# Unit zero of a gating stage: bf16 pieces turned by DMA in place of fp32 transposes and products on TensorE

## Chip, cores and metric

The kernel runs on one core of one Trainium2 chip. The metric is the device time of one execution in microseconds, the median of several runs; a profiled execution gives the trace that is read below.

## What is computed

Three stages follow each other: attention with a band and a few global keys, a dense feed-forward layer with SiLU, and a layer of eight experts of which each token uses one.

```python
x = attention(q, k, v, n_global, n_local)          # 2 x 768 tokens, 8 heads of 64 -> 1536 x 512
h = x @ w_in                                       # 512 -> 2048
x = (h * (1.0 / (1.0 + np.exp(-h)))) @ w_out       # 2048 -> 512
logits = x @ w_gate                                # 512 -> 8
e_idx = np.argmax(logits, axis=1)
probs = softmax(logits)
eom = 1.0 / (1.0 + np.exp(-(x @ w_output_gate)))
for e in range(8):
    mask = e_idx == e
    ye = np.maximum(x[mask] @ w1[e], 0.0) @ w2[e]
    out[mask] = probs[mask, e, None] * eom[mask, e, None] * ye
```

The change touches the step in the middle, the gate: the products of x with `w_gate` and `w_output_gate` (16 columns together). They decide by argmax which expert a token goes to, so they are needed with fp32's precision.

## The kernel before

The 1536 tokens are 12 tiles of 128. Two tiles make a unit, `u` = 0 to 5, and the units form five chunks, `CH=[[0,1],[2],[3],[4],[5]]`. The feed-forward layer runs over chunks, and in a chunk over `FB` = 16 slices `f` of the hidden width. The loop at L1091 has one step `g` for each (chunk, slice), 80 in all; a step issues the first product of its slice (`s1_mm`, L353), the activation (tanh on ScalarE at L357, VectorE at L358, a rounded copy on ScalarE at L361, the rest on VectorE at L362), and `LAG` = 2 steps later the second product (`s2_mm`, L373 to L375, the last with the low part of the weights, which for chunks after the first is loaded from DRAM by `load_wol`, L342).

Between these products a step carries pieces of other work, and all engines work through their instructions in the order in which the program wrote them (a schedule by hand):

- attention of later tiles, in slots of one head pair (`slot`): scores (L171), bias and maximum on VectorE (L182), exponentials on ScalarE (L192), a split into two halves (L196, L199), a DMA transpose of the probabilities (L202), and two or three slots later the product with the values, `emit_pv` (L252), into the single bank `pv`. After the last head pair of a tile VectorE copies the global rows of the values (`glob_v`, L163), scales the bank into SBUF (`emit_fin`, L262), and only then may the next tile write the bank. The values are split by ScalarE and GpSimd (L148 to L153);
- the gate of the units of the chunk that has ended, a list `gq` of small functions of which one is run in each step from step 18 on (L1114).

For a unit outside the set `PU` (L418) the list holds `gate1` for each of the two tiles (four fp32 transposes on TensorE, L415, and a copy by ScalarE, L417), `gate2` (fp32 logits on TensorE, L448; argmax on VectorE), `gate3` (rank of a token within its expert, two exponentials L486 and L487, the token's factor) and `gate4` (with `gate3` it scatters the two tiles' rows to DRAM from GpSimd's queue, L498). For a unit in `PU` the activations are split into three bf16 parts: `piece1` casts on ScalarE (L428), `piece2` subtracts on VectorE (L430), `piece3` casts (L432), `piece4` subtracts (L434), `turn` transposes a tile's parts with two DMA transposes on SyncE's queue (L437, L438), two empty entries follow, and `gate2` has 24 bf16 matmuls of 48 columns (L446) and one more reduction (L456). Units zero and one both end with chunk zero, so they stand in the list one after the other; after a unit in `PU` the next unit starts four entries before its end, and entries that meet are run in one step, the older first (L1128 to L1131). Unit one's turns are four entries of one DMA transpose each (L1125).

The parts' buffers are shared: the bf16 pairs are two buffers of tag `wt`, and units zero and one (two and three) share one tile `gx` (L422).

Of the kernel before, what the change touches and what calls it, by code (L numbers as in the profile page):

```python
# [23 lines left out]
def kernel(ctx, tc, qk, v, n_global, n_local, w_in, w_out, wg, w1, w2, out):  # L24
# [107 lines left out]
    def abank(shape,name):  # L132
        tg=atags[0][acnt[0]%len(atags[0])]; acnt[0]+=1
        return ps.tile(shape,F32,tag=tg,name=name,bufs=1)
# [277 lines left out]
    def gate1(n):  # L412
# [2 lines left out]
        for k in range(KC): T.transpose(m[:,k,:],xr[:,k*P:(k+1)*P],ident)  # L415
        x=mp.tile([P,KC,P],F32,tag="wt",name="xtf",bufs=2); xts[n]=x
        A.activation(out=x,in_=m,func=AF.Copy)  # L417
    PU=(1,2,3)  # L418
    gbuf={}; xps={}
    def piece1(u):  # L420

# [13 lines left out]
    def turn(n,part=(0,1)):  # L435
        a,b,r,x=xps[n]
        if 0 in part: S.dma_start_transpose(out=x[:,0:2].rearrange("p a k t -> p (a k) t"),in_=a.rearrange("p a d -> p (a d)"))  # L437
        if 1 in part: S.dma_start_transpose(out=x[:,2],in_=b); xts[n]=x; del xps[n]  # L438
    gsm={}
    glp={}  # L440
    def logits(n):
        if n%2==0: glp[n//2]=abank([P,2,48 if n//2 in PU else 16],"gl")
        x=xts.pop(n)
        if n//2 in PU:
            for i in range(3):
                for k in range(KC): T.matmul(glp[n//2][:,n%2],x[:,i,k,:],wgb[:,k].rearrange("p j e -> p (j e)"),start=(i==0 and k==0),stop=(i==2 and k==KC-1))  # L446
            return
        for k in range(KC): T.matmul(glp[n//2][:,n%2],x[:,k,:],wgs[:,k,:],start=(k==0),stop=(k==KC-1))  # L448
    def gate2(u):
# [4 lines left out]
        s=mp.tile([P,2,48],F32,tag="gsm",name="gsm",bufs=2)  # L454
        if u in PU:
            V.tensor_reduce(out=s[:,:,32:48],in_=g.rearrange("p t (j e) -> p t e j",j=3),axis=AX.X,op=ALU.add)  # L456
# [39 lines left out]
    def gate4(u,t):  # L496
        di,xr=gdi[u]
        G.indirect_dma_start(out=XE[:,:],out_offset=bass.IndirectOffsetOnAxis(ap=di[:,t:t+1],axis=0),in_=xr[:,t,:],in_offset=None,bounds_check=NE*CAP-1,oob_is_err=False)  # L498
# [562 lines left out]
    with tc.manual_schedule():  # L1061
# [27 lines left out]
        def run_gates(k):  # L1089
            for _ in range(min(k,len(gq))): gq.pop(0)()  # L1090
        for g in range(len(steps)+LAG):  # L1091
# [23 lines left out]
            if g>=LAG:  # L1115
                c2,f2=steps[g-LAG]
                s2_mm(c2,f2)
                if f2==FB-1:
# [4 lines left out]
                    for u in CH[c2]:  # L1123
                        seq=[lambda n=n,fn=turn if u in PU else gate1: fn(n) for n in (2*u,2*u+1)]
                        if u==1: seq=[lambda n=n,h=h: turn(n,(h,)) for n in (2,3) for h in (0,1)]  # L1125
                        if u in PU: seq=[lambda u=u,fn=fn: fn(u) for fn in (piece1,piece2,piece3,piece4)]+seq+[lambda: None]*2
                        seq+=[lambda u=u,fn=fn: fn(u) for fn in (gate2,gate3,lambda u: gate4(u,1))]
                        for i,fn in enumerate(seq):  # L1128
                            if at+i<len(gq): gq[at+i]=lambda fs=(gq[at+i],fn): [f() for f in fs]
                            else: gq.append(fn)  # L1130
                        at=len(gq)-(4 if u in PU else 0)  # L1131
                    run_gates(3 if c2==0 else 1)
# [75 lines left out]
```

## Time and profile before

| what | us |
|---|---|
| median of 3 runs | 571.04 (570.72 to 571.72) |
| the profiled execution, whole | 572.04 |
| its span, first to last instruction | 570.3 |

| engine | busy, us | share of the span |
|---|---|---|
| TensorE, matmuls | 555.1 | 97% |
| VectorE | 388.2 | 68% |
| ScalarE | 302.7 | 53% |
| GpSimd | 142.8 | 25% |

Times inside the execution are counted from the first instruction. Chunk zero ends near 144 us; the gate of units zero and one lies between 144 and 220. An instruction's row shows its start, its duration (or that of a merged run of equal ones), engine, line, operation and tiles, and in brackets how long the engine sat idle before it and what ended the idle time. Matmuls are pipelined, so the start of the next group tells better than the duration how long a group held TensorE.

### The profile page before, as it was taken

What the parts mean: (1) busy time and instruction counts of PE and PEld (TensorE: products, weight loads), DVE (VectorE), ACT (ScalarE), POOL (GpSimd) and SP (SyncE); (2) the same over time, 40 slices, a digit from 0 to 9 for tenths busy, and PEclk for the clock granted to TensorE, in tenths of its full rate; (3) what the DMA queues carried; (4) which work ended last, traced back from release to release, by engine and by line L of the source; (5) the groups of instructions that cost most, each with busy time, mean ns of one, the idle gap of its engine ahead of it and who ended that gap; (6) DMA issues with size and microseconds to landing.
All of it is one profiled execution on the core that took longest, in us unless ns stands there. A gap on an engine that the chain in (4) does not pass through costs nothing.

```text
span 570.3 us, 12006 instructions
## 1 busy us (share of the span) xinstructions
PE 555.1 (97%) x4027; PEld 469.6 (82%) x4027; DVE 388.2 (68%) x1143; ACT 302.7 (53%) x819; POOL 142.8 (25%) x193
## 2 busy tenths in 40 slices
PE   9999999999999999999999999999999999999993
PEld 4668998888888788888899998788888888888882
DVE  6996899996467657574735346656774967967950
ACT  7993434443545454434532425736655766877740
POOL 2686444343233323123201010220010110110011
PEclk9999999999999999999999999999999999999998
DMA  6876467796657985765493349309764868768500
GB/s 221 273 245 193 173 210 235 241 306 204 185 155 170 185 205 153 167 153 142 111 185 115 91 127 327 141 21 328 267 206 149 248 200 269 239 213 291 157 20 22
DMA packets 90731, 107.53 MB, mean 189 GB/s; under 512 B 39181, under 2 KB 53517, under 8 KB 90661
## 3 DMA queue, kind: packets, MB, share of 16 engines
q1 hardware_dynamic: 87892, 99.77, 58.8%
q0 software_dynamic: 2192, 6.39, 3.0%
q8 instruction: 33, 0.54, 0.4%
q10 hardware_dynamic: 576, 0.52, 0.3%
q14 instruction: 38, 0.30, 0.2%
HBM read 87.14 MB, written 17.66 MB: 184 GB/s over the span
## 4 chain that ended last, share of the span: by engine, by line
PE 87%; ACT 3%; DMA 3%; DVE 2%; issue 2%; POOL 1%; SPq 1%; POOLq 0%; ACTq 0%; DVEq 0%
PE s L353 21%; PE s L373 8%; PE s L374 7%; PE s L375 7%; PE h L696 7%; PE y L729 4%; PE h L697 4%; PE y L731 4%; PE y L730 4%; PE qkp L171 2%; PE pv L252 2%; PE h L702 2%; PE xy L171 2%; PE y L725 2%; PE px L228 1%
## 5 line engine op out<-in xcount | busy, mean ns | idle before, releaser
L353 PEld LDWEIGHTS s<-xT,wi 128*128 128x128 f32 x1152 | 147.6, 190 | 9.6 <-DVE g L362 3.8
L353 PE MATMUL s<-xT,wi 128*128 128x256 f32 x1152 | 151.6, 283 | 0.5 <-DVE g L362 0.5
L357 ACT ACTIVATE u<-s 128x256 f32<-128x256 f32 x96 | 35.4, 381 | 102.2 <-PE s L353 101.4
L358 DVE SCALAR_TENSOR_TENSOR s<-u,s 128x256 f32<-128x256 f32 x96 | 39.7, 426 | 67.3 <-ACT u L357 67.1
L373 PE MATMUL s<-woh,g 128*128 128x512 f32 x192 | 79.4, 414 | 0.4 <-ACT g L361 0.4
L567 DVE TENSOR_TENSOR uq<-qr,uq 128x512 fp32r<-128x512 f32 x112 | 74.4, 689 | 5.2 <-ACT uq L566 3.2
L374 PE MATMUL s<-woh,g 128*128 128x512 f32 x192 | 75.8, 395 | 0.0
L566 ACT ACTIVATE uq<-qr 128x512 fp32r<-128x512 f32 x112 | 66.6, 625 | 3.1 <-DMA qr<-in_w_dram 3.1
L362 DVE TENSOR_TENSOR g<-s,g 128x256 fp32r<-128x256 f32 x96 | 39.3, 422 | 31.1 <-ACT g L361 28.2
L653 POOL DMA_INDIRECT out_dram<-y,ixt x17 | 19.4, 1143 | 154.7 <-ACT y L742 116.4
L361 ACT ACTIVATE g<-s 128x256 fp32r<-128x256 f32 x96 | 35.6, 381 | 29.8 <-DVE s L358 29.8
L192 ACT ACTIVATE t<-t,mx 128x256 f32<-128x256 f32 (+1 forms) x96 | 46.1, 486 | 0.1
L373 PEld LDWEIGHTS s<-woh,g 128*128 128x128 f32 x192 | 36.3, 189 | 8.5 <-ACT u L357 2.7
L374 PEld LDWEIGHTS s<-woh,g 128*128 128x128 f32 x192 | 36.3, 189 | 5.5 <-DVE g L362 0.5
L375 PE MATMUL s<-wolr,g 128*128 128x512 f32 x128 | 39.8, 392 | 0.8 <-DMA wolr<-wlo_d 0.8
L709 DVE TENSOR_TENSOR h<-h,hs 128x192 f32<-128x192 f32 (+5 forms) x56 | 20.8, 372 | 25.3 <-ACT hs L708 25.2
L729 PE MATMUL y<-uq,hh 128*128 128x512 f32 (+1 forms) x88 | 36.7, 417 | 0.0
L730 PE MATMUL y<-uq,hh 128*128 128x512 f32 (+1 forms) x88 | 34.6, 393 | 0.0
L731 PE MATMUL y<-uq,hh 128*128 128x512 f32 (+1 forms) x88 | 34.6, 393 | 0.0
L711 ACT ACTIVATE hh<-h 128x192 fp32r<-128x192 f32 (+5 forms) x56 | 19.8, 353 | 26.3 <-DVE h L709 15.8
L199 POOL TENSOR_TENSOR hl<-t,hl 128x512 f16<-128x512 f32 (+1 forms) x18 | 19.9, 1105 | 50.4 <-ACT xT L276 16.4
L696 PE MATMUL h<-xwT,uq 128*128 128x448 f32 (+5 forms) x144 | 32.4, 347 | 0.0
(273 smaller groups left out, 1043.4 us busy)
## 6 DMA issues: line engine op xcount, KB each, us to landing
qr<-in_w_dram SPq DMA_DIRECT2D x128, 256.0 KB, 4.3
wolr<-wlo_d SPq DMA_DIRECT2D x64, 256.0 KB, 3.4
wiraw<-in_w_in_dram SPq DMA_DIRECT2D x16, 512.0 KB, 5.2
wraw<-in_w_out_dram SPq DMA_DIRECT2D x13, 512.0 KB, 4.2
ring<-in_qk_dram SPq DMA_DIRECT2D x22, 256.0 KB, 4.2
xe<-xe SPq DMA_DIRECT2D x7, 792.0 KB, 6.7
wlo_d<-wol SPq DMA_DIRECT2D x16, 256.0 KB, 3.0
xw<-xe SPq DMA_DIRECT2D x15, 264.0 KB, 4.7
```

Of the source, the lines that this page charges most:

```text
L192: A.activation(out=t[:,j,:ce],in_=t[:,j,:ce],func=AF.Exp,scale=-1.0 if 4*n<SB else 0.125,bias=mx[n][:,h:h+1],accum_out=ss[n][:,h,0:1])
L353: T.matmul(t,w[:,ww,kc,:],x[:,xx,kc,:],start=(k==0),stop=(k==11)); k+=1
L358: V.scalar_tensor_tensor(out=t,in0=u,scalar=1.0,in1=t,op0=ALU.add,op1=ALU.mult)
L373: T.matmul(o,g[u][:,0,sl],wh,start=(f==0),stop=False)
L374: T.matmul(o,g[u][:,1,sl],wh,start=False,stop=False)
L375: else: T.matmul(o,g[u][:,0,sl],wl,start=False,stop=(f==FB-1))
L566: A.activation(out=t[:,0],in_=r,func=AF.Copy)
L567: (G if (i%2 if pool is None else pool) else V).tensor_tensor(out=t[:,1],in0=r,in1=t[:,0],op=ALU.subtract)
L696: for kc in range(KC): T.matmul(t[:,:2*W],uq[4*p+2*(f//4),kc][:,0,s],xwT[p,kc][:,:,:W],start=(kc==0),stop=False)
L729: T.matmul(o,hi,w[:,0],start=(f==0),stop=False)
L730: T.matmul(o,g[:,z:z+n],w[:,0],start=False,stop=False)
L731: T.matmul(o,hi,w[:,1],start=False,stop=(f==7))
```

## The change

Unit zero joins the set `PU`. `turn` takes the place of `gate1` for its two tiles, its logits are the 24 bf16 matmuls, and the list of entries is built by the same lines as for the other units of the set. Units four and five keep the fp32 form.

```diff
-    PU=(1,2,3)
+    PU=(0,1,2,3)
```

The lines that read the set, unchanged:

```python
if u in PU: seq=[lambda u=u,fn=fn: fn(u) for fn in (piece1,piece2,piece3,piece4)]+seq+[lambda: None]*2
...
at=len(gq)-(4 if u in PU else 0)
```

## Rows read from the trace of the kernel before

**Rows 1.** Page, part 1: busy time, share of the span, instructions.

```profile
PE 555.1 (97%) x4027; PEld 469.6 (82%) x4027; DVE 388.2 (68%) x1143; ACT 302.7 (53%) x819; POOL 142.8 (25%) x193
```

**Rows 2.** Timeline of PE, unit zero's transposes and logits: start, us, engine, line.

```profile
145.61 0.66 PE L415 MATMUL gt<-ident,xr 128*128 128x128 f32 x4
146.03 0.48 PE L373 MATMUL s<-woh,g 128*128 128x512 f32 x1
...
153.28 1.96 PE L448 MATMUL gl<-wgs,xtf 128*128 128x16 f32 x16
155.09 0.48 PE L373 MATMUL s<-woh,g 128*128 128x512 f32 x1
```

**Rows 3.** Timeline of PE, unit one's bf16 logits.

```profile
207.62 0.76 PE L446 MATMUL gl<-wgb,gx 128*128 128x48 bf16 x24
208.23 0.48 PE L373 MATMUL s<-woh,g 128*128 128x512 f32 x1
```

**Rows 4.** Timeline of DVE: unit one's piece2, first and next after gate2, gate3.

```profile
171.62 1.28 DVE L430 TENSOR_TENSOR gx<-xr,xpa 128x512 f32<-128x512 f32 x2
...
210.06 0.25 DVE L456 TENSOR_REDUCE gsm<-gl 128x32 f32<-128x96 f32 x1
...
211.80 0.43 DVE L358 SCALAR_TENSOR_TENSOR s<-u,s 128x256 f32<-128x256 f32 x1
...
213.91 0.17 DVE L479 TENSOR_TENSOR gsm<-gr,geb 128x16 f32<-128x16 f32 x1
...
215.59 0.43 DVE L358 SCALAR_TENSOR_TENSOR s<-u,s 128x256 f32<-128x256 f32 x1
```

**Rows 5.** Windows: length, then busy time of PE, PEld, DVE, ACT, POOL.

```profile
180.30:194.40 14.10, 14.10 (x138) 11.52 (x137) 10.19 (x37) 6.45 (x22) 5.28 (x5) 1.00 0.90 195
```

**Rows 6.** Timeline of DVE, steps 26 to 29, and a later L163.

```profile
180.30 1.24 DVE L434 TENSOR_TENSOR xpb<-gx,xpa 128x512 bf16<-128x512 f32 x1
...
185.95 0.43 DVE L358 SCALAR_TENSOR_TENSOR s<-u,s 128x256 f32<-128x256 f32 x1 [1.29 <-ACT u L357]
...
187.72 0.43 DVE L362 TENSOR_TENSOR g<-s,g 128x256 fp32r<-128x256 f32 x1 [1.00 <-ACT g L361]
...
193.24 0.54 DVE L163 COPY vpr<-vpr 32x1536 bf16<-32x1536 bf16 x1
193.71 0.67 DVE L262 TENSOR_TENSOR xa<-pv,rs 128x512 f32<-128x512 f32 x1
...
217.23 1.82 DVE L163 COPY vpr<-vpr 32x1536 bf16<-32x1536 bf16 x1
```

**Rows 7.** Timeline of ACT: unit one's casts, a tanh, and gate3's second Exp.

```profile
174.85 1.14 ACT L432 ACTIVATE xpa<-gx 128x512 bf16<-128x512 f32 x2
...
185.54 0.38 ACT L357 ACTIVATE u<-s 128x256 f32<-128x256 f32 x1 [2.52 <-PE s L353]
...
214.64 0.21 ACT L487 ACTIVATE gsm<-gsm 128x2 f32<-128x2 f32 x1 [1.00 <-DVE gsm L485]
```

**Rows 8.** Timeline of PE at three places in chunk one.

```profile
178.19 0.47 PE L373 MATMUL s<-woh,g 128*128 128x512 f32 x1
...
195.30 0.76 PE L252 MATMUL pv<-vpr,pT 128*128 128x64 bf16 x20 [0.81 <-DVE mx L182]
...
213.03 0.63 PE L375 MATMUL s<-wolr,g 128*128 128x512 f32 x2
```

**Rows 9.** Tile gx: its DMA transposes, ns min/median/max on the queue; time to landing.

```profile
L437 SPq DMA_TRANSPOSE gx<-xpa x6: 1231/1296/1765, 187.7 to 292.1; - x6
...
DMA to landing us min/median/max: 2.7/3.3/5.0
```

**Rows 10.** Timeline of SyncE's queue: loads of the weights' low part.

```profile
167.72 0.38 SPq L342 DMA_DIRECT2D wolr<-wlo_d  x1
...
206.39 1.51 SPq L342 DMA_DIRECT2D wolr<-wlo_d  x3
```

**Rows 11.** Timeline of POOL: a unit's second scatter.

```profile
219.46 0.99 POOL L498 DMA_INDIRECT xe<-xr,gdi  x1 [0.83 <-DMA xe<-xr,gdi]
```

## The prediction

> **What bounds the kernel now.** First the busy shares: TensorE works in 555.1 of 570.3 us [rows 1], so a microsecond taken from its queue counts unless something else is made late. Second the timeline of TensorE at the two kinds of gating: unit zero's fp32 gate as three blocks of work, and unit one's bf16 gate as one [rows 2, 3]. Third the queues of VectorE, ScalarE and SyncE around them, since the change moves work there; what matters in them is not how busy they are but which wait ends last, and the place to watch is the one in chunk one where TensorE already stops, at the probability-times-value product `pv` of a new token tile [rows 8]. I count time in steps g of the unit loop. The gating entries run one per step from step 18 on; step 26 is the one whose `s1_mm` starts at 175 us, and each step after it takes about 4.2 us.
>
> **What is removed and added on TensorE.** Before, in steps 18 and 19 four fp32 transposes each hold TensorE from 145.61 to 146.03, 0.42 us, twice 0.84. In step 20 sixteen fp32 logit instructions hold it from 153.28 to 155.09, 1.81 [rows 2]. Sum removed 2.65 us. Added in step 26: 24 bf16 matmuls, priced by the same 24 of unit one, 207.62 to 208.23, 0.61 us [rows 3]. The six short matmuls of `gate3` move from step 21 to 27 and cost the same. **TensorE's own gain is 2.65 - 0.61 = 2.04 us.** As far as TensorE alone sets the end, the whole 2.04 reaches it.
>
> **What moves.** After the change unit zero takes the entries piece1 to piece4 (steps 18 to 21), turn 0 and turn 1 (22, 23), two empty ones (24, 25), then gate2, gate3 and gate4. The list lets the next unit start four entries before the end, so unit one's piece1 falls into step 25, its piece2 into step 26 with gate2 of unit zero, piece3 into 27 with gate3, piece4 into 28 with gate4. Unit one's turns go from steps 27 to 30 to steps 29 to 32, its gate2 from 33 to 35, and unit two comes two steps later throughout; from step 49 on the list is as before.
>
> **Steps 18 to 21.** ScalarE loses two PSUM copies and gains four casts, 1.14 us a pair [rows 7]; VectorE gains 1.28 us of subtractions in step 19 [rows 4] and some 1.9 (1.24 [rows 6] and a shorter one) in step 21, where gate3 took 1.68 until now. The consumer of what they push back, the second product, comes two steps later; I cost this at nothing, with some 4 us of cover, and if the cover failed the price would be the pair's own 1.1 to 1.9 us.
>
> **Steps 26 to 29, where the gain is given back.** VectorE's queue gets three blocks that weren't there: gate2 1.74 us (210.06 to 211.80), piece2 1.28, gate3 1.68 (213.91 to 215.59) [rows 4], 4.7 us; piece4 (from 180.30) only moves from step 26 to 28. In the 14.1 us from 180.30 to the end of `emit_fin` (L262, 193.71 and 0.67) VectorE is busy 10.19 [rows 5, 6], so 3.9 are idle: 1.29 for the tanh in step 28 and 1.00 for ScalarE's copy L361 in the same step [rows 6], and a like pair in step 29. If all of that could be filled, and with the 0.61 by which TensorE is later itself, VectorE would end about 0.2 late. It can't all be filled. In step 27 gate3 starts on VectorE at about 180.30 + 1.74 + 1.28 + 2.5 = 185.8 (2.5 is its usual work of that step: from the end of piece4, near 182.2, to 184.66, where the idle 1.29 begins [rows 6]); ScalarE's second Exp L487 waits for it, 0.73 after its start [rows 4, 7], so to 186.5; behind it on ScalarE stand L487's own 0.21, piece3's two casts, 1.14, and the tanh of step 28, 0.38 [rows 7], which ends at 188.1, while VectorE is free at 187.5: 0.6 idle. The 1.00 before L362 in step 28 stays too, because ScalarE has exponentials and a cast between the tanh and L361. So from 180.30: 10.2 + 4.7 + 1.6 + 0.3 of small gaps = 16.8, and L262 ends at 197.1 on the clock of before, that is 194.4 with the 2.65 saved ahead of it. The `pv` behind it writes the bank that L262 reads, so it can't start sooner; before it started at 195.30 [rows 8]. **At that point 0.9 us of the 2.04 are left**: TensorE waits 2.0 us there, where it waited 0.81. The bounds of that wait: 0.2 with all gaps filled (gain then 2.65) and 3.3 if L163, the copy ahead of L262, takes the 1.82 of another of its executions for its 0.54 [rows 6] (gain then -0.4). I take 2.0, as the row 193.24 has the same neighbours.
>
> On that copy: L163 took 0.54 us once and 1.82 once [rows 6], with GpSimd's subtraction beside it. The Trainium skill, SBUF — State Buffer, Who interferes with whom, says that such a VectorE copy and GpSimd hold a shared port pair in turn, whoever issues first, for the whole instruction; by that the sum would be the -0.4 just given if GpSimd came first.
>
> **SyncE.** Unit zero adds four DMA transposes, two each in steps 22 and 23, 1.30 us of the queue apiece (1.23 to 1.77) and 3.3 to landing (2.7 to 5.0) [rows 9]. Queued behind turn 0 stands the load of the weights' low part, 167.72, used three to four steps later [rows 10], then a ring load and the next tile's transpose of the probabilities. By the rows turn 0 fills 167.7 to 170.3, those three go to 172.6, turn 1 takes 172.6 to 175.2, and its second part, issued at 173.9, lands at 177.2; gate2 of unit zero would have its place on TensorE at 178.19, where L373 starts in step 26 [rows 8]. 1.0 us of cover, so nothing; with a landing of 5.0 it is a wait of 0.7. Another wait is added on ScalarE: piece1 of unit one writes the buffers that turns 0 and 1 read, and its second cast, at about 175.4 [rows 7], must wait for the landing of turn 1's first part, 172.6 + 3.3 = 175.9. Behind it is the tanh of step 26, due near 176.7: the second cast still ends before it; with 5.0, the tanh and all VectorE work behind it are 1.4 late. In step 32 two more transposes stand before the three loads of the next chunk (206.39 [rows 10]), whose first is used at 213.03 [rows 8]; with a transpose in step 31 too, some 4 us later on the queue against 2 on TensorE, which leaves cover of about 1 or none. On GpSimd the two scatters of unit zero, 1.0 us each with 0.83 of waiting for the one before [rows 11], now stand before the value splits of steps 28 and 29, which then end a microsecond before the `pv` that uses them: nothing. For all these small ones together I take **0.3 us lost**, between -0.3 and 1.5.
>
> **The sum.** -2.65 + 0.61 + 1.2 (the wait at `pv` from 0.81 to 2.0) + 0.3 = -0.54 us. The profiled execution took 572.04 us with its span of 570.3, 1.0 over the median of the runs; the same step from it gives 571.5 for a profiled execution, and from the median 571.04 the forecast 570.5.
>
> **Rivals.** *VectorE catches up.* Its idle time in steps 27 to 29 takes the blocks, the wait at `pv` stays near 0.8 or goes: gain 2.04 to 2.6, time 568.5 to 569.0, with some small loss up to 569.9. For it speaks that 3.9 us are idle there; against it the order on ScalarE, in which piece3 stands behind an Exp that waits for VectorE. *The transposes come late for gate2 of unit zero.* Four at 1.77 put turn 1's second part 1.9 later, and a landing of 5.0 another 1.7: it lands at 180.8, TensorE waits 2.6 us at 178.19, and with the wait at `pv` the sum is -2.04 + 1.2 + 2.6 = +1.8, time 572.8. It outweighs the gain of 0.84 from a landing at 179.0 on, and shows as slower from 180.2 on. For it speaks that steps 22 and 23 carry six transposes where unit one's four lie in four steps; against it that the median on the queue is 1.30. The Trainium skill, VectorE: DVE Perf Modes, Rules for kernel authors, advises TensorE for a 128x128 transpose whose result may go to PSUM, and DMA otherwise; that is this rival's side, and the rows agree (four TensorE transposes 0.42 us, one DMA transpose 1.30 of its queue and 3.3 to landing), but TensorE is the engine that is full here. *The change doesn't do what it says*: the set is read by the logits, by gate2 and by the order of the entries alike, so I leave it no chance.
>
> **How the numbers follow.** 0.2% of the time is 1.14 us, about what a measurement of this kernel can tell from no change. The forecast, gain between -1.1 and 1.1, has 0.50; the first rival 0.32; the second 0.18. Range: the lower end 568.6 takes in nearly all of the first rival, the upper end 572.4 half of the second; the forecast's own range is 569.9 to 572.2.
>
> **What would show it.** Right: no fp32 transposes at 145 to 150; the 24 short matmuls near 175.4 with no wait before them; steps of VectorE near 178 to 194 without idle time but for some 1.6 us; TensorE waiting about 2 us before `pv` at about 194.4; from there the same kernel, 0.5 to 0.9 earlier. Wrong: no wait, or one under 1 us, at that `pv` (first rival); a wait before the 24 matmuls (second); or a stop at the low-part product of the next chunk's first step.

## The result, and the profile after

The changed kernel takes 574.83 us, the median of 17 executions (571.57 to 578.42), against 571.6 for the kernel before in 17 executions beside them: a ratio of 1.0054 with the 95% interval 1.0036 to 1.0071. It is slower, and above the range of the prediction (568.6 to 572.4). The profiled execution took 578.42 us with a span of 576.6, 6.3 more than the span of before, while the medians lie 3.2 apart; the sums below are made against the profiled ones, since only they leave rows.

Part 1 of the page of after, in the columns of [rows 1]: TensorE works 1.3 us longer though it was given less to do, and works for a smaller share of the span.

```profile
PE 556.4 (96%) x4027; PEld 470.1 (82%) x4027; DVE 391.9 (68%) x1148; ACT 304.0 (53%) x821; POOL 142.1 (25%) x193
```

Where the time goes is seen best from the starts of `s1_mm` (L353) on TensorE's timeline, one per step:

| step g | before, us | after, us | after minus before |
|---|---|---|---|
| 17, ahead of all edits | 139.49 | 140.20 | +0.7 |
| 26 | 175.03 | 173.37 | -1.7 |
| 30 | 192.26 | 191.52 | -0.7 |
| 31 | 197.76 | 202.64 | +4.9 |
| 32 | 201.96 | 207.46 | +5.5 |
| 35 | 213.50 | 219.53 | +6.0 |
| 47 | 258.36 | 265.20 | +6.8 |
| end of the span | 570.3 | 576.6 | +6.3 |

Up to step 30 the kernel gains as forecast in kind, but less: 2.4 us between steps 17 and 26, of which 0.9 go back for the logits and the rank's matmuls in steps 26 and 27, so that 1.5 of the 2.04 are left. One step then loses 5.6 us. Timeline of TensorE of after (start, us, engine, line, operation, tiles; in brackets how long the engine was idle before and what ended that):

```profile
176.65 0.76 PE L446 MATMUL gl<-wgb,gx 128*128 128x48 bf16 x24
...
198.15 1.23 PE L252 MATMUL pv<-vpr,pT 128*128 128x64 bf16 x20 [4.35 <-DVE xa L262]
...
202.64 2.21 PE L353 MATMUL s<-xT,wi 128*128 128x256 f32 x12
...
218.97 0.73 PE L375 MATMUL s<-wolr,g 128*128 128x512 f32 x2 [1.01 <-DMA wolr<-wlo_d]
...
226.46 0.18 PE L475 MATMUL gr<-geb,upper 128*128 128x8 bf16 x1 [0.60 <-DVE geb L467]
```

The 24 logit matmuls of unit zero have no wait before them. The wait at `pv`, 0.81 in [rows 8], is 4.35. Behind it the same instructions take longer: the 20 `pv` matmuls 1.23 for 0.76, `s1_mm` 2.21 for some 1.6. The windows of after say why (length, busy time of PE, PEld, DVE, ACT, POOL with counts, then the granted TensorE clock):

```profile
192.00:196.00 4.00, 1.80 (x14) 1.36 (x13) 3.85 (x11) 1.86 (x6) 2.19 (x3) 1.00 1.06 201
196.00:200.00 4.00, 1.85 (x25) 1.85 (x24) 3.85 (x10) 0.38 (x1) 1.08 (x1) 0.65 0.45 86
200.00:204.00 4.00, 4.00 (x15) 3.42 (x14) 0.97 (x3) 0.60 (x1) 1.17 (x1) 0.50 0.95 217
204.00:208.00 4.00, 4.00 (x42) 3.29 (x42) 2.13 (x11) 1.63 (x6) 0.00 (x0) 1.00 0.41 65
```

TensorE is idle for more than half of each of the first two windows. The granted clock is 0.65 of full speed in the second and 0.50 in the third, which is the lower of its two levels, 1.2 GHz, and from 204 on it is full again. Before, all three windows from 192 to 204 show 1.00.

Why TensorE waits is read from VectorE and GpSimd, around the place of [rows 6]. VectorE of after:

```profile
187.16 0.43 DVE L358 SCALAR_TENSOR_TENSOR s<-u,s 128x256 f32<-128x256 f32 x1 [0.65 <-ACT u L357]
...
188.94 0.42 DVE L362 TENSOR_TENSOR g<-s,g 128x256 fp32r<-128x256 f32 x1 [1.01 <-ACT g L361]
...
194.48 3.02 DVE L163 COPY vpr<-vpr 32x1536 bf16<-32x1536 bf16 x1
197.43 0.67 DVE L262 TENSOR_TENSOR xa<-pv,rs 128x512 f32<-128x512 f32 x1
```

GpSimd of after in the same stretch:

```profile
187.48 1.17 POOL L498 DMA_INDIRECT xe<-xr,gdi  x1 [0.71 <-POOL xr L492]
188.73 1.15 POOL L149 TENSOR_TENSOR vraw<-vraw,vpr 128x512 f32<-128x512 f32 x1
193.79 0.99 POOL L498 DMA_INDIRECT xe<-xr,gdi  x1 [3.91 <-DMA xe<-xr,gdi]
194.81 1.17 POOL L153 TENSOR_TENSOR vpr<-vraw,vpr 128x512 bf16<-128x512 f32 x1
195.92 1.16 POOL L199 TENSOR_TENSOR hl<-t,hl 128x512 f16<-128x512 f32 x1
```

The second scatter of unit zero waits 3.91 us for the first one, where [rows 11] had 0.83: it starts 6.3 us after it, there 3.0 (216.43 and 219.46). Behind it in GpSimd's queue stand L153 and L199, so that three GpSimd instructions run without a gap from 193.79 to 197.08. VectorE, late from its extra blocks, comes to the copy L163 at 194.48, while the scatter still runs. The copy takes 3.02 us, where it took 0.54 in [rows 6], and ends 0.42 after L199 does.

The theory from these rows: **GpSimd's wait pushes its work onto VectorE's copy, the copy makes `pv` late, and the long stop costs TensorE a stretch at the lower clock.** The sum against the profiled execution: -2.04 on TensorE (the forecast; the table shows 1.5 up to step 30), +3.54 at `pv` (4.35 less 0.81), +2.65 at the lower clock (from the start of `pv` to `s1_mm` of step 31 it is 4.49 us against 2.46, and to that of step 32 another 4.82 against 4.20), +1.01 for the low part's load and -0.22 at a later one (0.55 at 362.06; 0.77 at 355.30 before), +0.34 for the rank's matmul (0.60; 0.26 for unit two's before), and +0.71 that this execution was late before any edit: 6.0 of 6.3. The rivals: that VectorE's blocks alone make it late, that the two-step shift of units one and two costs by itself, or that the copy itself is at fault.

### The profile page after: what moved, and what is told of

Its sections match the earlier page's. It is cut to its first block, busy times and chain, and to the rows that moved or that the text cites. A ratio compares the mean times of both kernels' runs of the same rounds, so it can differ in the third digit from the quotient of the medians.

```text
span 576.6 us, 12015 instructions
## 1 busy us (share of the span) xinstructions
PE 556.4 (96%) x4027; PEld 470.1 (82%) x4027; DVE 391.9 (68%) x1148; ACT 304.0 (53%) x821; POOL 142.1 (25%) x193
## 4 chain that ended last, share of the span: by engine, by line
PE 57%; DVE 13%; issue 12%; DMA 8%; ACT 5%; POOL 3%; SPq 1%; POOLq 0%; DVEq 0%; ACTq 0%
PE s L353 8%; PE h L696 7%; PE y L729 4%; PE h L697 4%; PE y L730 4%; PE y L731 4%; PE s L373 3%; DMA xe<-xr,gdi 3%; PE s L375 3%; DVE dct L301 3%; PE s L374 3%; DVE wt L303 2%; DVE dct L302 2%; PE h L702 2%; PE xy L171 2%
## 5 line engine op out<-in xcount | busy, mean ns | idle before, releaser
L353 PEld LDWEIGHTS s<-xT,wi 128*128 128x128 f32 x1152 | 148.5, 191 | 9.7 <-DVE g L362 3.8
L353 PE MATMUL s<-xT,wi 128*128 128x256 f32 x1152 | 152.3, 284 | 0.5 <-DVE g L362 0.5
L358 DVE SCALAR_TENSOR_TENSOR s<-u,s 128x256 f32<-128x256 f32 x96 | 39.7, 425 | 71.2 <-ACT u L357 71.2
L362 DVE TENSOR_TENSOR g<-s,g 128x256 fp32r<-128x256 f32 x96 | 39.2, 422 | 29.6 <-ACT g L361 26.4
L199 POOL TENSOR_TENSOR hl<-t,hl 128x512 f16<-128x512 f32 (+1 forms) x18 | 19.8, 1100 | 60.6 <-ACT xT L276 15.4
```

The source lines that it names most:

```text
L353: T.matmul(t,w[:,ww,kc,:],x[:,xx,kc,:],start=(k==0),stop=(k==11)); k+=1
L358: V.scalar_tensor_tensor(out=t,in0=u,scalar=1.0,in1=t,op0=ALU.add,op1=ALU.mult)
```

## The experiments

All ratios are against the kernel before, run on the same chip. Diffs are against the changed kernel, except where the text says otherwise.

**GpSimd's scatters moved away.** Unit zero's two scatters get entries of their own, at the ends of steps 29 and 30, behind the value splits; everything else keeps its step.

```diff
-        gate4(u,0)
+        if u: gate4(u,0)
...
-  seq+=[lambda u=u,fn=fn: fn(u) for fn in (gate2,gate3,lambda u: gate4(u,1))]
+  if u: seq+=[lambda u=u,fn=fn: fn(u) for fn in (gate2,gate3,lambda u: gate4(u,1))]
+  else: seq+=[lambda: gate2(0),lambda: gate3(0),lambda: None,lambda: gate4(0,0),lambda: gate4(0,1)]
...
-  at=len(gq)-(4 if u in PU else 0)
+  at=len(gq)-((4 if u else 6) if u in PU else 0)
```

> The changed kernel with one edit: unit zero's two scatters on GpSimd come at the ends of steps 29 and 30, behind the value split L153 and the subtraction L199 of step 29, and no longer ahead of them. Theory (GpSimd's order): in the changed kernel the second scatter waits 3.91 us for the first, so L153 and L199 run just when VectorE's copy L163 wants to, L163 takes 3.02 us, TensorE waits 4.35 us at pv and runs at half its granted clock for some 6 us behind it. Here L163 should take 0.5 to 1 us, the wait at pv fall to 2 us or less, the clock stay at 1.00 in that stretch, and the time be 570 to 571.5, ratio to before 0.997 to 1.001. Rival (VectorE's load alone, the blocks of unit zero and one in the same steps): L163 gets shorter or not, but the wait stays over 3 us with the half clock behind it, ratio 1.004 to 1.007.

Measured: 574.3 us, ratio 1.0045 [1.002, 1.0071]. TensorE's two waits, then VectorE's copy:

```profile
195.44 0.74 PE L252 MATMUL pv<-vpr,pT 128*128 128x64 bf16 x20 [1.65 <-DVE xa L262]
...
214.89 0.98 PE L375 MATMUL s<-wolr,g 128*128 128x512 f32 x2 [2.23 <-DMA wolr<-wlo_d]
```

```profile
194.25 0.54 DVE L163 COPY vpr<-vpr 32x1536 bf16<-32x1536 bf16 x1
```

At `pv` the theory holds: the copy takes 0.54 again, the wait falls from 4.35 to 1.65, and the clock stays at 1.00 from 188 to 212. But the time hardly falls. The stop has moved to the next chunk's first low-part product. The windows there, in the columns above:

```profile
212.00:216.00 4.00, 1.77 (x7) 1.16 (x6) 0.60 (x3) 1.15 (x4) 1.15 (x1) 0.90 1.15 203
216.00:220.00 4.00, 4.00 (x58) 3.86 (x57) 1.02 (x5) 0.77 (x2) 0.00 (x0) 0.67 0.56 166
```

SyncE's queue shows what delays the load: two transposes of unit one and a ring load stand ahead of it, so that it is issued at 209.70, where before it was issued at 206.39 [rows 10].

```profile
206.36 1.27 SPq L437 DMA_TRANSPOSE gx<-xpa  x1
207.68 0.59 SPq L140 DMA_DIRECT2D ring<-in_qk_dram  x1
208.32 1.29 SPq L438 DMA_TRANSPOSE gx<-gx  x1
209.70 1.53 SPq L342 DMA_DIRECT2D wolr<-wlo_d  x3
```

So the cause at `pv` is confirmed, and a second one stood behind it, hidden as long as TensorE was late for another reason: in the changed kernel this wait was 1.01.

**The units apart.** Unit one's entries begin when unit zero's have ended, so VectorE has one block a step; the scatters stay where the change put them.

```diff
-  at=len(gq)-(4 if u in PU else 0)
+  at=len(gq)-(4 if u in PU and u else 0)
```

> The changed kernel with one edit: unit one's entries begin only when unit zero's are over (step 29), so no step has the blocks of both; the later units come four steps later than in the changed kernel. Theory (blocks of both units in steps 26 to 28 make VectorE late for L262): no wait over 0.9 us at pv in step 30, full clock there, and the 2.04 us saved on TensorE reach the end: 569 to 570, ratio 0.995 to 0.998. Rival (unit zero's DMA transposes or the later place of the other units cost the time): ratio 1.000 or more, with new waits of TensorE in chunk two or at the low-part loads.

Measured: 572.08 us, ratio 1.0001 [0.9981, 1.0022], missing the gain expected. TensorE and GpSimd:

```profile
194.24 0.38 PE L252 MATMUL pv<-vpr,pT 128*128 128x64 bf16 x7 [1.07 <-DMA pT<-hl]
195.30 0.85 PE L252 MATMUL pv<-vpr,pT 128*128 128x64 bf16 x13 [0.68 <-POOL vpr L153]
```

```profile
193.06 0.99 POOL L498 DMA_INDIRECT xe<-xr,gdi  x1 [4.70 <-DMA xe<-xr,gdi]
194.08 1.17 POOL L153 TENSOR_TENSOR vpr<-vraw,vpr 128x512 bf16<-128x512 f32 x1
```

VectorE reaches the copy in time here (0.54 at 191.92, L262 at 192.38), and between 165 and 235 TensorE has no wait for the low part's loads. Yet the second scatter still waits, now 4.70 us, and holds back the value split L153, for which the second half of `pv` itself waits. The two stops of 1.07 and 0.68 us lie close together, and the granted clock falls to 0.90 and 0.68 in the windows from 192 to 200. The scatters therefore cost without VectorE's lateness too, 0.68 us of it through the values. The stop of 1.07 is a wait for the transposed probabilities: VectorE made them late, because its TENSOR_SCALAR L185 took 1.19 us at 187.20 for its usual 0.17, beside the GpSimd instruction right behind the first scatter (L149, 187.19 to 188.36), and their transpose, issued at 189.47, then took 4.8 us to land; no run separates the two.

**The copy on ScalarE.**

```diff
-        else: V.tensor_copy(vpr[0:32,n%3],vpr[0:32,(n-1)%3])
+        else: A.activation(out=vpr[0:32,n%3],in_=vpr[0:32,(n-1)%3],func=AF.Copy)
```

> The changed kernel with one edit: the copy of the global value rows L163 (chunks one to three) is done by ScalarE, about 1.4 us each, in place of VectorE. Theory (GpSimd's order): L262 is no longer held behind the copy and ends near 195, but pv also reads the value split L153, which GpSimd finishes only near 196 because of the scatter ahead of it; so the wait at pv falls from 4.35 to about 2.2 us, the granted clock drops for less long or not at all, ratio 0.999 to 1.003. Rival (VectorE's copy is the only thing that holds pv): the wait falls to 1.4 us or less, ratio 0.996 to 0.999. Rival (VectorE's load without the copy): the wait stays over 3 us.

Measured: 573.35 us, ratio 1.003 [1.001, 1.0049]. The wait at `pv` is 2.92 where 2.2 was expected, and it is VectorE again that ends it: L262 ends at 196.14, L153 at 195.08. Without the copy, another VectorE instruction meets GpSimd's work, one of 128 x 2 numbers that takes 0.17 us elsewhere:

```profile
193.34 1.78 DVE L185 TENSOR_SCALAR mx<-mx 128x2 f32<-128x2 f32 x1
```

```profile
193.91 1.17 POOL L153 TENSOR_TENSOR vpr<-vraw,vpr 128x512 bf16<-128x512 f32 x1
```

It begins while the second scatter runs (192.90 to 193.89) and ends at 195.12, as L153 does at 195.08. So the copy is not special: another small instruction of VectorE can be held until GpSimd's is over. Not every one is: L182's, at 192.88 beside the same scatter, took its usual 0.41. The clock is 0.57 from 196 to 200.

**TensorE kept busy through the stop.** (Line numbers are three higher here.) 14 bf16 matmuls of 512 columns on constants, into a spare bank, ahead of the `pv` of the first head pair of tile 8. They add work and take nothing away.

```diff
+    def filler(k):
+        m=abank([P,512],"fl")
+        for _ in range(k): T.matmul(m.rearrange("p (a b) -> p a b",a=4),ones,ones[:,None,:].to_broadcast([P,4,P]),start=True,stop=True)
...
+                if (n3,h3)==(8,0): filler(14)
```

> The changed kernel with one edit: ahead of the pv product that waits in step 30, TensorE does 14 bf16 matmuls of 128x512 on constants into a scratch bank (about 3.1 us of its time at full clock), which fill the greater part of its wait; nothing reads them. Theory (the half clock behind the wait costs 3 us of its own): the wait is 1 to 1.5 us, the granted clock stays 1.00, and the time is some 3 us under that of the changed kernel: 571 to 572.5, ratio 0.999 to 1.002. Rival (the wait itself costs all of it, the clock little): ratio 1.004 to 1.007, as without the filler.

Measured: 573.22 us, ratio 1.0038 [1.002, 1.0055]. The filler runs from 194.92 to 197.94, no wait is left at `pv`, and the clock stays full:

```profile
194.92 3.18 PE L86 MATMUL fl<-ones 128*128 128x512 bf16 x14
197.94 0.75 PE L255 MATMUL pv<-vpr,pT 128*128 128x64 bf16 x20
```

```profile
196.00:200.00 4.00, 3.91 (x38) 2.60 (x37) 3.84 (x14) 2.01 (x6) 1.80 (x2) 1.00 0.36 112
```

From `s1_mm` of step 30 to that of 31 it is 7.9 us, against 11.1 in the changed kernel. Not all of the 3.2 us is the clock's: in this execution the copy took 0.54 and a 128 x 2 TENSOR_SCALAR ahead of it 1.44, and `pv` started 5.2 us after `s1_mm` of step 30 instead of 6.6. What is the clock's is the stretch behind: 2.72 us from the start of `pv` to the next `s1_mm`, against 4.49 in the changed kernel and 2.46 before. That is 1.8 us bought with work that computes nothing. The ratio fell by less than expected: the waits at the low part (1.21) and at the rank's matmul (0.59) were still there, and this execution had one of 1.64 at the low-part product of step 18 (148.34), ahead of the filler. The interval overlaps that of the changed kernel, so the time by itself does not show what the filler did; the rows do, and so does the mean granted clock of each execution, 0.994 to 0.997 in all ten, against 0.988 to 0.995 (median 0.992) in the 17 of the changed kernel.

**The shift alone.** The kernel before, with fp32 for unit zero, and two empty entries ahead of unit one: units one and two come two steps later as in the change.

```diff
+  if u==1: seq=[lambda: None]*2+seq
```

> The kernel before with one edit: two empty entries ahead of unit one, so that it and unit two come two steps later, as in the changed kernel; unit zero stays fp32. Theory (DMA transposes of unit one in steps 31 and 32 stand ahead of the loads of the weights' low part for chunk two): TensorE waits 0.5 to 2 us at the low-part product of step 34, with a half clock behind it if the wait is near 2; ratio to before 1.001 to 1.005. Rival (only unit zero's own blocks and scatters cost, the later place of unit one nothing): ratio 0.999 to 1.001 and no wait at that product over 0.3 us.

Measured: 570.72 us, ratio 0.9996 [0.9981, 1.0012]; the theory that the shift costs by itself falls. The low part's wait comes, at the low end of what was expected (0.43 for 0.5 to 2), but costs nothing in sum. The shift removes the wait at `pv` (0.81 before) and adds two in the next chunk:

```profile
211.84 0.73 PE L375 MATMUL s<-wolr,g 128*128 128x512 f32 x2 [0.43 <-DMA wolr<-wlo_d]
...
219.32 0.18 PE L475 MATMUL gr<-geb,upper 128*128 128x8 bf16 x1 [0.59 <-DVE geb L467]
```

**Both edits.** The changed kernel with the scatters moved to the ends of steps 29 and 30 and unit one begun later (in the first diff, 6 becomes 2 and 4 stays for the other units).

```diff
-  at=len(gq)-(4 if u in PU else 0)
+  at=len(gq)-((4 if u else 2) if u in PU else 0)
```

> The changed kernel with both edits together: unit one begins when unit zero is over (its transposes then come after the loads of the low part), and unit zero's scatters come at the ends of steps 29 and 30, behind the value split. Theory (the loss is made of three waits that follow from the order: VectorE late for L262, GpSimd's scatter ahead of the value split, transposes ahead of the low-part loads, and of the half clock behind such waits): none of the three waits over 1 us, full clock from 180 to 300, 569 to 570, ratio 0.995 to 0.998. Rival (the bf16 form of unit zero costs by itself, wherever it stands): ratio 1.000 or more.

Measured: 568.26 us (568.06 to 569.43), ratio 0.9951 [0.9934, 0.9969], faster than both kernels. TensorE's timeline has no wait between 130 and 260, the clock is 1.00 in every window from 188 to 224, and the copy takes 0.54 at 191.82. GpSimd's value split and unit zero's two scatters:

```profile
190.28 1.17 POOL L153 TENSOR_TENSOR vpr<-vraw,vpr 128x512 bf16<-128x512 f32 x1 [2.86 <-ACT vpr L152]
...
193.56 1.18 POOL L498 DMA_INDIRECT xe<-xr,gdi  x1 [0.18 <-DVE s L358]
...
198.12 0.99 POOL L498 DMA_INDIRECT xe<-xr,gdi  x1 [1.31 <-DMA xe<-xr,gdi]
```

The value split comes ahead of the scatters, and the second scatter, with other work between, waits 1.31. The span is 566.4, 3.9 below that of before: the 2.04 saved on TensorE, and the waits of 0.81, 0.77 and 0.26 of the kernel before, which are gone too. By the ratio of the executions the gain is 2.8 us (1.8 to 3.8), so that the sum of 3.9 holds for the profiled pair and lies at the upper end for all.

**The transpose behind the load.** The first experiment, with unit one's last transpose one step later, behind the low part's loads; one of the two empty entries goes.

```diff
+  if u==1: seq=seq[:3]+[lambda: None]+seq[3:]
-  if u in PU: seq=[lambda u=u,fn=fn: fn(u) for fn in (piece1,piece2,piece3,piece4)]+seq+[lambda: None]*2
+  if u in PU: seq=[lambda u=u,fn=fn: fn(u) for fn in (piece1,piece2,piece3,piece4)]+seq+[lambda: None]*(1 if u==1 else 2)
```

> The kernel with unit zero's scatters late (as in the first experiment) and one more edit: unit one's last DMA transpose comes one step later, in step 33, behind the loads of the low part and not ahead of them; an empty entry behind it is dropped, so gate2 stays in step 35. Theory (the two transposes ahead of these loads make the wait of 2.23 us at the low-part product of step 34): that wait falls under 0.8 us, no half clock at 212 to 220, the wait at pv in step 30 stays near 1.6; ratio 0.997 to 1.000. Rival (the loads land late because the DMA engines are full there, whatever stands ahead of them): the wait stays over 1.5 us, ratio 1.003 to 1.006.

Measured: 571.58 us, ratio 1.0002 [0.9986, 1.0019], just over the range expected and 0.43% below the first experiment.

```profile
195.64 0.74 PE L252 MATMUL pv<-vpr,pT 128*128 128x64 bf16 x20 [1.86 <-DVE xa L262]
...
213.34 0.74 PE L375 MATMUL s<-wolr,g 128*128 128x512 f32 x2 [0.57 <-DMA wolr<-wlo_d]
```

The loads' wait falls from 2.23 to 0.57 and the clock stays full. What is left over the version with both edits is 1.86 at `pv`, 0.57 here, 0.28 before unit one's logits (for a transpose, now late) and 0.16 at the rank, 2.87 together; the times differ by 0.51%, 2.9 us.

**The changed kernel once more.**

> The changed kernel once more, one look: does the order of the three waits repeat? Theory (fixed by the order of the instructions): TensorE waits over 2.5 us at pv in step 30, L163 or another VectorE instruction beside it is stretched by GpSimd to over 1 us, the second scatter waits over 3 us, half clock behind; the low-part product waits 0.5 to 2.5 us. Rival (a chance of one execution): the wait is near the 2.0 us of the forecast and the clock stays full.

Measured: 577.76 us in the profiled execution. The same three rows, in TensorE, VectorE and GpSimd:

```profile
198.70 1.22 PE L252 MATMUL pv<-vpr,pT 128*128 128x64 bf16 x20 [4.42 <-DVE xa L262]
```

```profile
194.96 3.09 DVE L163 COPY vpr<-vpr 32x1536 bf16<-32x1536 bf16 x1
```

```profile
194.33 1.01 POOL L498 DMA_INDIRECT xe<-xr,gdi  x1 [3.96 <-DMA xe<-xr,gdi]
```

The clock is 0.61 and 0.54 from 196 to 204. The wait at the low part is 0.49, at the lower edge of what was expected, and there is one of 0.80 at the low-part product of step 18.

**The four together.** The ratios of the two edits, alone and both:

| | scatters as changed | scatters late |
|---|---|---|
| unit one as changed | 1.0054 | 1.0045 |
| units apart | 1.0001 | 0.9951 |

Moving the scatters is worth 0.1% (within the noise) or 0.5%, taking the units apart 0.5% or 0.9%, each more when the other is done, because each leaves a stop that the other removes. Taking the units apart does two things at once: it frees VectorE in steps 26 to 28 and takes unit one's last transposes from in front of the loads. The transpose experiment separates these: the transposes 0.4%, VectorE and the small waits 0.5%.

## Why the prediction was wrong, step by step

**TensorE's own gain: right in its terms, somewhat large.** The fp32 transposes and logits are gone, and the 24 matmuls cost what unit one's cost. From step 17 to 28, ahead of all stops at `pv`, the gain is 1.46 us in the changed kernel and 1.65 with both edits, for 2.04; in the spans of the profiled pair, with both edits, it is all there.

**Steps 18 to 21 at nothing: right in what it names.** TensorE gains 2.4 us from step 17 to 26, where 2.65 were forecast. Most of the difference lies in step 18: its low-part product, now 0.42 earlier, comes about when its load lands. That costs 0.3 in this execution, and TensorE waits there for the load 0.22, 0.80 and 1.64 us in others of the changed kernels, which the prediction did not look for.

**The order on ScalarE and VectorE: right.** The second Exp L487 waits for VectorE, piece3 stands behind it, and VectorE idles for the two gaps named: 0.65 before L358 (forecast 0.6) and 1.01 before L362 (1.00). So does the wait for turn 1 on ScalarE's second cast. ScalarE of after:

```profile
174.90 0.63 ACT L428 ACTIVATE xpa<-xr 128x512 bf16<-128x512 f32 x1 [1.10 <-DMA gx<-xpa]
...
185.62 0.21 ACT L487 ACTIVATE gsm<-gsm 128x2 f32<-128x2 f32 x1 [2.74 <-DVE gsm L485]
```

The wait of 2.0 us at `pv` that follows from it is what the kernels show in which the scatters are out of the way: 1.65 and 1.86.

**GpSimd at nothing: wrong, and the first step that failed.** The text took 0.83 us for the second scatter's wait, from [rows 11], and let both scatters end a microsecond ahead of `pv`. That row is of another place. From 216 to 220 in the kernel before the DMA engines are busy 0.22 of the time, and in after 0.77 from 188 to 192, with loads for chunk one and attention:

```profile
216.00:220.00 4.00, 4.00 (x25) 3.19 (x25) 3.96 (x11) 1.72 (x6) 2.73 (x3) 1.00 0.22 78
```

```profile
188.00:192.00 4.00, 4.00 (x43) 3.29 (x42) 2.96 (x9) 2.91 (x10) 1.81 (x2) 1.00 0.77 264
```

(The first is of before, the second of after; the last two numbers are the DMA share and GB/s.) That the busy engines are what makes the first scatter slower is the likely reading; no run took the loads away. In the five executions with the scatters in this place the wait was 3.91, 3.96, 3.66, 3.31 and 4.70. No bound was put on it, and the instructions behind it on GpSimd (L153, L199) were counted as late for `pv` only, not as coming upon VectorE.

**The copy L163 at 0.54: wrong, and the step that carries most.** The prediction had named it, given both durations of [rows 6] and said what the longer one would make of the wait (3.3); it then chose 0.54 "as the row 193.24 has the same neighbours". The change moved those neighbours. The copy took 3.02, more than the bound of 1.82.

The trace of before had the rule for it. GpSimd beside the copy at 193.24, beside that at 217.23 [rows 6], and beside a third:

```profile
193.31 1.49 POOL L199 TENSOR_TENSOR hl<-t,hl 128x512 f16<-128x512 f32 x1 [0.43 <-DVE hl L196]
...
216.43 1.00 POOL L498 DMA_INDIRECT xe<-xr,gdi  x1 [0.63 <-DMA wolr<-wlo_d]
217.44 1.19 POOL L199 TENSOR_TENSOR hl<-t,hl 128x512 f16<-128x512 f32 x1
...
245.90 1.17 POOL L199 TENSOR_TENSOR hl<-t,hl 128x512 f16<-128x512 f32 x1 [2.31 <-DVE hl L196]
```

```profile
246.16 1.32 DVE L163 COPY vpr<-vpr 32x1536 bf16<-32x1536 bf16 x1
```

The prediction showed two of the copy's four executions; the others took 1.32 and 1.41 (276.22, beside a GpSimd instruction that began at 276.05), so 0.54 was the exception. It is the one in which the copy began first, by 0.07 us, and there GpSimd's instruction took 1.49 for 1.17. The other three began while GpSimd was at work and ended 0.41 to 0.42 after it. The copy of 1.82 began inside a scatter and outlasted the instruction behind it too, and so did those of 3.02 and 3.09, with two instructions behind the scatter. So the step that failed is the choice of the row: what was needed was whether the copy would begin ahead of GpSimd's run of instructions, and when that run would end. The Trainium skill, SBUF — State Buffer, Who interferes with whom, says that a VectorE instruction of this kind and a GpSimd one hold a shared port pair in turn and that the one to start first keeps it for the whole instruction. The trace agrees in both directions (0.54 with 1.49, and 1.32 with 1.17). It shows beyond this that GpSimd instructions without a gap between them hold the copy up together.

**The clock behind a stop: left out.** 2.65 us of the 6.3. The prediction counted a wait at its own length only. With the wait of 0.81 in [rows 8] the clock had stayed at 1.00, and nothing of before showed a longer stop in this stage.

**SyncE's small terms: the mechanism right, the size off.** The wait at the low part of the next chunk's first step was named, as cover "of about 1 or none", and put into a term of 0.3 for all. It measured 1.01, and 2.23 once TensorE came on time: outside the bound of 1.5 by itself. With it the clock fell too.

**The rivals.** The transposes were not late for gate2 of unit zero (no wait before the 24 matmuls at 176.65). The first rival, VectorE catching up, did not happen either, for the gaps on ScalarE that spoke against it. Slower was given 0.18 by a mechanism that did not occur; the one that did, GpSimd's late work meeting VectorE's, stood in the text as two separate small doubts and as no rival.

What stays open: how much of the loss the shorter executions of the changed kernel have (571.57 to 578.42; the version with both edits spreads over 1.4 us), since no rows of them exist. The two that left rows are long ones, 578.42 and 577.76 against a median of 574.83, so the sum of 6.0 us is theirs and not that of the median's 3.2. The mean granted clock, known for all, is lower on the whole: 0.988 to 0.995 with a median of 0.992, against 0.992 to 0.997 with a median of 0.995 for the kernel before, beside the experiments.

## What to carry to other kernels

When a step is moved to where other work stands, take the price of its wait from what will stand there, not from another place, and follow each queue that is pushed: which instruction of a third engine will now run beside it. A duration that differs between two rows of the same instruction is a sign of a neighbour; look at all its executions, ask which of the two began first in each, and where the neighbour goes after the change, before one of the durations is chosen. And price a stop of TensorE by more than its length where the trace has no stop as long that left the clock alone.

## What the hardware showed that was not expected

- **The granted clock behind a stop.** Stops of 4.35 and 4.42 us were followed by windows at 0.65 and 0.50, and 0.61 and 0.54; 2.92 by one at 0.57; 2.23 by 0.67; two stops of 1.07 and 0.68 close together by 0.68. Behind stops of 0.81, 1.01, 1.21, 1.64, 1.65 and 1.86 the windows show 1.00. In the changed kernel this added 2.65 us to a wait that was 3.54 longer.
- **A scatter waits for the one before it** from 0.83 [rows 11] to 4.70 us, and GpSimd's queue stands still meanwhile. It started 3.0 us after the first in the kernel before, 4.6 with both edits, 6.3 in after and 7.1 with the units apart.
- **GpSimd's instructions hold up VectorE's small ones.** The copy of 32 x 1536 took 0.54 us when it began ahead of GpSimd's instruction, which then took 1.49 for 1.17. Begun while GpSimd was at work it ended 0.41 to 0.42 us after the last of GpSimd's instructions that followed without a gap: 1.32 and 1.41 with one, 1.82 with a scatter and one, 3.02 and 3.09 with a scatter and two. An instruction on 128 x 2 numbers took 1.19, 1.44 and 1.78 for 0.17, and each time ended within 0.04 us of GpSimd's.
